# Choosing the step of a 64-row tile by where a run of score banks stands, and short runs in the first block

## The chip, the cores and the metric

One core of a Trainium2 chip runs the whole program. The metric is the time of one execution on the device, in microseconds (us), lower is better. Each kernel was run several times beside the kernel before on the same chip.

Words used throughout: **PE** is TensorE, **ACT** ScalarE, **DVE** VectorE. A *step* is the use of one key group (four tiles of 128 keys) for one query *block* (512 queries, six blocks in a batch, six steps in a block, eight batches, 288 steps). A *score unit* is half a group: two 64-row matmuls into one pair of PSUM banks, one ACT pass (relu and scale), one DVE square. A *run* is the score units issued one after the other within a step. The *tail* is the last key tile, which has only 64 rows. *Mixer work* is the MLP of the batch before, filled in between.

## The reference, cut to what matters

```python
scores = (1 / S) * z @ z.T                      # S = 3008, 64 features
attn   = maximum(scores, 0) ** 2
x      = u * (attn @ v)                         # 3008 x 256 for each of 8 batches
u2     = x + (relu(x.T @ w_tok1) @ w_tok2).T    # token mixing
out    = u2 + relu(u2 @ w_ch1) @ w_ch2          # channel mixing
```

Scores are symmetric: outside the first batch only key groups g >= q are computed ("direct"), the others come from a transposed copy.

## The kernel before: the parts that matter

Scores contract over 64 rows, so two matmuls share the array on its two halves. The tail does the same: its two output halves are computed side by side from the two copies of 64 rows. Everything else uses all 128 rows.

```python
BURST = 3
def burst(us):                      # a run: score matmuls on PE, then ACT; returns the squares
    for (b, q, g), pr in us:
        sc = psum.tile([P, 2, QW], F32, tag="ps", name="sc", bufs=3)
        for r in range(2):          # two 64-row matmuls, one on each half of the array
            nc.tensor.matmul(sc[:, r, :W], zT[h, ...], zT[h, ...])
    ...
    nc.scalar.activation(view, sv, ACT.Relu, scale=inv_S)
    return [lambda u=u, v=v: square(u, v) for u, v in zip(us, views)]   # DVE

def key_order(b, q):                # before: the tail's group (NG-1) has a fixed place
    direct = [g for g in range(NG) if direct_block(b, q, g)]
    if q == 0:
        return direct if b == 0 else [direct[0], direct[-1]] + direct[1:-1]
    direct = [direct[-1]] + direct[:-1]
    ...                             # then direct and transposed groups in turn

for n, (b, q, g) in enumerate(groups):
    def due(used):                  # are the next groups' scores running short?
        return ahead < len(units) and ahead < (used + 2) * (GK // 2)
    used += direct_block(b, q, g)
    if n and due(used):
        squares = burst(units[ahead:ahead + BURST]); ahead += BURST
    pre, half = av(b, q, g, first, last)
    for f in pre: f()               # the tail pair, if this is the tail's group
    if n and not last:
        for f in squares: f()
    half(0)                         # products into accumulator 0
    if last: gate(b, q, 0)          # DVE: accumulator 0 times u
    ...                             # mixer work
    half(1)                         # products into accumulator 1
    if last:
        gate(b, q, 1)
        for f in squares: f()       # in a block's last step the squares stand behind both gates
    ...
```

## Time and profile before

| | before |
|---|---|
| median of 4 runs (lowest to highest) | 1239.66 us (1238.43 to 1240.38) |
| PE busy | 97% of the span |
| DVE / ACT busy | 49% / 40% |
| granted PE clock, mean | 0.996 |

PE is the bound. Its busy time cannot be read as work, because a matmul's end is modelled and a 0.38 us bar covers the short waits behind it. I go by the time from one matmul's start to the next one's.

### The profile page before, as it was taken

Reading aid. Unit: us, or ns where it says so; the run is one execution under the profiler, and the core shown is the slowest. Engines: PE = TensorE matmul, PEld = TensorE weight load, DVE = VectorE, ACT = ScalarE, POOL = GpSimd, SP = SyncE. Lnnn points to the kernel's source line nnn. Section 1 sums busy time; section 2 is a strip of 40 time slices with the busy share of each in tenths; the row PEclk is TensorE's granted clock in tenths of the full one; section 3 lists DMA queues with packets and bytes.
Section 4 is the critical chain, followed back from the end, with each engine's and each line's share of the span. In section 5 each row is a group of like instructions: output and inputs, shape, how many; then the busy total and the mean of one; then the engine's idle time right before and its main releaser. Section 6 shows DMA issues by size and latency. Waiting matters only on the chain.

```text
span 1238.4 us, 17322 instructions
## 1 busy us (share of the span) xinstructions
PE 1198.6 (97%) x7089; PEld 631.8 (51%) x7089; DVE 605.8 (49%) x781; ACT 493.8 (40%) x521; POOL 144.4 (12%) x272
## 2 busy tenths in 40 slices
PE   6999999999999999999999999999999999999998
PEld 2334455554555555464545545555455554555566
DVE  3665644436444365435454355543653436443443
ACT  4776443333433334323443244423434334332022
POOL 2542010110101001011001111011010110000000
PEclk8999999999999999999999999999999999999999
DMA  8999955897657967689576876578965897544132
GB/s 140 139 140 171 159 113 105 141 163 146 110 119 132 173 118 133 123 132 175 103 125 128 157 137 125 114 148 154 147 112 102 147 165 139 110 85 86 33 77 67
DMA packets 438400, 157.73 MB, mean 127 GB/s; under 512 B 402288, under 2 KB 415920, under 8 KB 438320
## 3 DMA queue, kind: packets, MB, share of 16 engines
q1 hardware_dynamic: 410464, 123.92, 52.5%
q0 software_dynamic: 27344, 32.32, 19.0%
q8 instruction: 55, 0.90, 0.3%
q10 hardware_dynamic: 512, 0.38, 0.1%
q14 instruction: 25, 0.20, 0.1%
HBM read 65.40 MB, written 24.64 MB: 73 GB/s over the span
## 4 chain that ended last, share of the span: by engine, by line
PE 79%; ACT 9%; DVE 5%; issue 4%; DMA 3%; SPq 0%; POOL 0%; DVEq 0%; ACTq 0%; POOLq 0%
PE acc L304 34%; PE hp L393 18%; PE op L411 18%; ACT at L260 6%; PE sc L242 5%; DVE xT L376 3%; ACT h2pre L400 3%; PE a_ps L358 3%; DMA zT<-zr 1%; DVE xT L330 1%; DMA u_sb<-xT 1%; DMA fl<-at 1%; PE h_ps L372 1%; DVE h2pre L398 0%; DMA x_sb<-xT 0%
## 5 line engine op out<-in xcount | busy, mean ns | idle before, releaser
L260 ACT ACTIVATE at<-sc 128x1024 bf16<-128x1024 f32 (+1 forms) x366 | 342.9, 1023 | 369.0 <-PE sc L242 369.0
L304 PE MATMUL acc<-at,v_sb 128*128 128x512 bf16 (+3 forms) x1464 | 359.2, 380 | 6.3 <-DVE xT L330 5.4
L265 DVE TENSOR_TENSOR at<-at 128x1024 bf16<-128x1024 bf16 (+1 forms) x366 | 250.2, 701 | 209.8 <-ACT at L260 208.1
L304 PEld LDWEIGHTS <-v_sb 128*128 128x128 bf16 (+1 forms) x2304 | 208.0, 98 | 270.9 <-issue 77.9
L411 PE MATMUL op<-w_ch_sb,h2pre 128*128 128x256 bf16 (+1 forms) x2304 | 277.9, 273 | 5.9 <-ACT h2pre L400 2.8
L400 ACT ACTIVATE h2pre<-hp 128x1024 bf16<-128x1024 f32 (+1 forms) x144 | 145.1, 1007 | 314.6 <-PE hp L393 314.6
L393 PE MATMUL hp<-xT,w_ch_sb 128*128 128x512 bf16 (+1 forms) x1152 | 266.8, 375 | 2.6 <-ACT h2pre L400 2.3
L411 PEld LDWEIGHTS <-h2pre 128*128 128x128 bf16 (+1 forms) x2304 | 223.1, 98 | 66.1 <-ACT h2pre L400 13.0
L398 DVE TENSOR_SCALAR h2pre<-hp 128x1024 bf16<-128x1024 f32 (+1 forms) x144 | 171.8, 1199 | 77.9 <-PE hp L393 77.5
L304 PE MATMUL acc<-fl,v_sb 128*128 128x512 bf16 (+1 forms) x840 | 193.5, 370 | 0.0
L393 PEld LDWEIGHTS <-w_ch_sb 128*128 128x128 bf16 x1152 | 112.6, 98 | 133.1 <-issue 5.6
L419 DVE TENSOR_TENSOR res<-op,u_sb 128x512 f32<-128x512 f32 x88 | 60.9, 692 | 222.4 <-PE op L411 184.1
L242 PE MATMUL sc<-zT 64*128 64x512 bf16 (+1 forms) x732 | 107.4, 381 | 16.3 <-DMA zT<-zr 7.2
L330 DVE TENSOR_TENSOR xT<-acc,uT 128x512 bf16<-128x512 f32 (+1 forms) x96 | 63.9, 668 | 70.9 <-PE acc L304 69.6
L242 PEld LDWEIGHTS <-zT 64*128 64x128 bf16 x732 | 30.1, 94 | 94.4 <-issue 72.4
L147 POOL DMA_DIRECT2D ur<-in_u_dram x48 | 26.0, 543 | 419.2 <-DMA uT<-ur 411.5
L97 POOL COPY zr<-zs 128x512 bf16<-128x512 bf16 x42 | 27.0, 644 | 343.6 <-DMA zT<-zr 343.3
L376 DVE TENSOR_TENSOR xT<-xT,h_ps 128x1024 bf16<-128x1024 bf16 (+1 forms) x48 | 53.9, 1192 | 14.0 <-PE h_ps L372 14.0
L372 PE MATMUL h_ps<-w_tok_sb,a_sb 128*128 128x512 bf16 (+1 forms) x192 | 43.3, 374 | 1.5 <-ACT a_sb L364 0.7
L358 PE MATMUL a_ps<-x_sb,w_tok_sb 128*128 128x256 bf16 x384 | 43.7, 273 | 1.0 <-DMA x_sb<-xT 1.0
L137 POOL DMA_DIRECT2D v_sb<-in_v_dram x48 | 25.9, 543 | 143.7 <-PE acc L304 136.8
L358 PEld LDWEIGHTS <-w_tok_sb 128*128 128x128 bf16 x384 | 37.6, 98 | 7.6 <-issue 1.2
(34 smaller groups left out, 115.3 us busy)
## 6 DMA issues: line engine op xcount, KB each, us to landing
out_dram<-res SPq DMA_DIRECT2D x88, 256.0 KB, 2.3
v_sb<-in_v_dram POOLq DMA_DIRECT2D x40, 256.0 KB, 5.3
ur<-in_u_dram POOLq DMA_DIRECT2D x40, 256.0 KB, 5.6
zs<-in_z_dram POOLq DMA_DIRECT2D x35, 64.0 KB, 4.0
fl<-at SPq DMA_TRANSPOSE x105, 4.6
v_sb<-in_v_dram POOLq DMA_DIRECT2D x8, 192.0 KB, 5.1
w_ch_sb<-in_moe_w_ch_dram POOLq DMA_DIRECT2D x4, 384.0 KB, 5.6
ur<-in_u_dram POOLq DMA_DIRECT2D x8, 192.0 KB, 3.3
```

Of the source, the lines that this page charges most:

```text
L242: nc.tensor.matmul(sc[:, r, :W], zT[h, k * P:(k + 1) * P], zT[h, q * QW:q * QW + W], start=True, stop=True)
L260: nc.scalar.activation(view, sv, ACT.Relu, scale=inv_S)
L265: nc.vector.tensor_mul(view, view, view)
L304: nc.tensor.matmul(o, vt[rows, i, dh * P:(dh + 1) * P], rhs, start=st, stop=sp, skip_group_check=True)
L330: nc.vector.tensor_mul(xT[:, dh, :full * P].rearrange("p (t s) -> p t s", s=P), acc[:, :full * P].rearrange("p (t s) -> p t s", s=P), uT[: ...
L358: nc.tensor.matmul(st["a_ps"][:, th, :], w_tok1_sb[:, k, th * P:(th + 1) * P], x[:, :, i, :], start=(k == 0 and th == 0), stop=(k == KT - ...
L376: nc.vector.tensor_add(xT[:, :, :W], xT[:, :, :W], h[:, :, :W])
L393: nc.tensor.matmul(hp[:, r, :W], w_ch1_sb[:, dc, cc * P:(cc + 1) * P], xT[:, dc, :W], start=(dc == 0), stop=(dc == DT - 1))
L398: nc.vector.tensor_single_scalar(h2[:, :, :W], hp[:, :, :W], 0.0, AX.max)
L400: nc.scalar.activation(h2[:, :, :W], hp[:, :, :W], ACT.Relu)
L411: nc.tensor.matmul(op[:rows[i], i, :], st["h2", q, cc // 2][:, cc % 2, c0:c0 + rows[i]], w_ch2_sb[:, cc, :], start=(cc == 0 and i == 0), s ...
L419: nc.vector.tensor_add(res.rearrange("p i (h d) -> p i h d", d=P), op.rearrange("p i (h d) -> p i h d", d=P), us[:, :, half * 2:half * 2 + ...
```

## The change

Its intent: PE pays for each change between 128-row and 64-row use, so put the tail directly behind a run of score matmuls, which is in 64-row mode already. For that the tail's group loses its fixed place: it is taken at the first step where its two units have been issued and a run is due. The first block gets runs of two, so that a run does not ask for a key group whose z has not arrived. Core of the diff, with cuts marked:

```diff
+    def made(b, q):                 # order in which the score units are made
+        gs = [g for g in range(LAST) if direct_block(b, q, g)]
+        return gs if (b, q) == (0, 0) else gs[:1] + [LAST] + gs[1:]
...
-    for f in burst(units[:BURST]):
+    for f in burst(units[:2]) + burst(units[2:4]):
         f()
...
-    ahead = BURST
+    ahead = 4
...
+    def choose(n, used):
+        b, q = n // NB, n % NB // NG
+        todo = left.setdefault((b, q), key_order(b, q) + [LAST])
+        if n < NG:
+            return todo[0], 0 < n
+        tail = (b, q, LAST)
+        if LAST in todo and place[tail] * 2 + 2 <= ahead and due(used + 1):
+            return LAST, True
+        return todo[0], due(used + direct_block(b, q, todo[0]))
...
-        if n and due(used):
-            squares = burst(units[ahead:ahead + BURST])
-            ahead += BURST
+        if now:
+            size = 2 if n < NG else BURST
+            squares = burst(units[ahead:ahead + size])
+            ahead += size
...
-        if n == 0:
-            for f in burst(units[ahead:ahead + BURST]):
-                f()
-            ahead += BURST
```

The buffer of squared scores also goes from five to six copies, and the scores of the tail's group are as a rule made second in their block.

More of the change, by code (lines that the diff above doesn't have):

```diff
@@ L208, in direct_block @@
         return b == 0 or g >= q
+    LAST = NG - 1
+    def made(b, q):
+        gs = [g for g in range(LAST) if direct_block(b, q, g)]
+        return gs if (b, q) == (0, 0) else gs[:1] + [LAST] + gs[1:]
     def key_order(b, q):
-        direct = [g for g in range(NG) if direct_block(b, q, g)]
-        if q == 0:
-            return direct if b == 0 else [direct[0], direct[-1]] + direct[1:-1]
-        direct = [direct[-1]] + direct[:-1]
-        flipped = [g for g in range(NG) if not direct_block(b, q, g)]
+        direct = [g for g in made(b, q) if g < LAST]
+        flipped = [g for g in range(LAST) if not direct_block(b, q, g)]
         order = []
@@ L222, in key_order @@
         return order
-    groups = [(b, q, g) for b in range(B) for q in range(NQ) for g in key_order(b, q)]
-    directs = [t for t in groups if direct_block(*t)]
+    directs = [(b, q, g) for b in range(B) for q in range(NQ)
+               for g in made(b, q) + ([LAST] if (b, q) == (0, 0) else [])]
+    place = {t: i for i, t in enumerate(directs)}
     units = [(t, pr) for t in directs for pr in range(GK // 2)]
@@ L249, in burst @@
             if pr == 0:
-                ats[b, q, g] = sb.tile([P, GK * QW], BF16, tag="at", name="at", bufs=5)
+                ats[b, q, g] = sb.tile([P, GK * QW], BF16, tag="at", name="at", bufs=6)
             at = ats[b, q, g]
@@ L453, in new_zT @@
         zTs[b] = sb.tile([P, KT, P], BF16, tag="zT", name="zT", bufs=2)
-    vorder = key_order(1, 0)
+    vorder = [0, LAST] + list(range(1, LAST))
     new_zT(0)
@@ L535, in mix, with due @@
             budget -= w.cost
-    for n, (b, q, g) in enumerate(groups):
+    NB = NQ * NG
+    left = {}
+    def due(used):
+        return ahead < len(units) and ahead < (used + 2) * (GK // 2)
+    def choose(n, used):
[7 more added lines that the diff above has]
+        return todo[0], due(used + direct_block(b, q, todo[0]))
+    for n in range(B * NB):
+        b, q = n // NB, n % NB // NG
         for f in fetch.get(n, []):
@@ L541 @@
         t = 1.73
-        def due(used):
-            return ahead < len(units) and ahead < (used + 2) * (GK // 2)
+        g, now = choose(n, used)
+        left[b, q].remove(g)
         squares = []
         used += direct_block(b, q, g)
-        if n and due(used):
-            squares = burst(units[ahead:ahead + BURST])
-            ahead += BURST
+        if now:
+            size = 2 if n < NG else BURST
+            squares = burst(units[ahead:ahead + size])
+            ahead += size
             t += 0.42 * BURST * 0.8
@@ L553 @@
         got = budget
-        soon = n + 1 < len(groups) and due(used + direct_block(*groups[n + 1]))
+        soon = n + 1 < B * NB and choose(n + 1, used)[1]
         pre, half = av(b, q, g, first, last)
```

## The prediction

> **What bounds the kernel now.** I read the page first (busy shares, slices, groups), then the groups kept apart by shape, then the timeline at three places: the start, and two steps at which the group with the 64-row tile is used.
>
> ```profile
> PE 1198.6 (97%) x7089; PEld 631.8 (51%) x7089; DVE 605.8 (49%) x781; ACT 493.8 (40%) x521; POOL 144.4 (12%) x272
> ...
> PE   6999999999999999999999999999999999999998
> ```
>
> TensorE is busy 97% of the span in program order; VectorE and ScalarE are half idle. Only the first slice (31 us) has a visible hole. So time is gained only where TensorE waits or works badly, and any wait put into its stream is paid in full. Modelled ends hide short waits, so I go by start-to-start times: a warm 512-column matmul follows another after 0.216 us, a 448-column one after 0.189, a pair of 64-row matmuls on the two halves costs one such time.
>
> ```profile
> 643.36 1.03 PE L393 MATMUL hp<-xT,w_ch_sb 128*128 128x512 bf16 x4
> 644.32 1.14 PE L304 MATMUL acc<-at,v_sb 64*128 64x512 bf16 x5
> 645.30 1.03 PE L393 MATMUL hp<-xT,w_ch_sb 128*128 128x512 bf16 x4
> ```
>
> The tail (two 64-row matmuls side by side) with three full matmuls behind it. Four full matmuls should take 0.864 us; 643.36 to 644.32 is 0.96, so the way into 64-row mode costs 0.096. From 644.32 to 645.30 one pair and three matmuls should again be 0.864 and take 0.98: the way back costs about 0.1. **A run of 64-row matmuls costs about 0.195 us besides its work.** Single records say the same: 0.312 instead of 0.216 going in, 0.305 to 0.319 coming out.
>
> The second cost stands where the tail opens a query block. It writes both accumulators at once; the second is free only when the previous block's second gate (L330) is done.
>
> ```profile
> 577.84 0.69 DVE L330 TENSOR_TENSOR xT<-acc,uT 128x512 bf16<-128x512 f32 x1 [0.73 <-PE acc L304]
> 578.60 0.10 PEld L304 LDWEIGHTS <-v_sb 64*128 64x128 bf16 x2 [0.42 <-issue]
> 578.71 0.69 DVE L330 TENSOR_TENSOR xT<-acc,uT 128x512 bf16<-128x512 f32 x1 [0.17 <-PE acc L304]
> 579.31 1.89 DVE L265 TENSOR_TENSOR at<-at 128x1024 bf16<-128x1024 bf16 x3
> 579.45 1.34 PE L304 MATMUL acc<-at,v_sb 64*128 64x512 bf16 x5 [0.46 <-DVE xT L330]
> ```
>
> No score run stands here. The first tail matmul starts with its weights at 578.60, its partner at 579.45: 0.85 us lost. Only now do the **squares** of the previous step's run start (579.31): in the last step of a block the program puts them behind both gates.
>
> ```profile
> 168.24 0.82 PE L242 MATMUL sc<-zT 64*128 64x512 bf16 x6
> 168.35 0.69 DVE L330 TENSOR_TENSOR xT<-acc,uT 128x512 bf16<-128x512 f32 x1 [0.17 <-PE acc L304]
> ...
> 168.90 1.32 PE L304 MATMUL acc<-at,v_sb 64*128 64x512 bf16 x5
> 168.95 3.09 DVE L265 TENSOR_TENSOR at<-at 128x1024 bf16<-128x1024 bf16 x5
> ```
>
> Here a run of three banks comes first and hides most of the gate: the tail pair is 0.19 us apart. Five squares take 3.09 us: 0.60 start to start, 0.68 for the last one.
>
> **What the Trainium skill says.** "TensorEngine Tiling (Array Packing)", Key Properties: changing the tiling mode drains the TensorE. The trace agrees: 0.096 in, about 0.1 out. "TensorE: Matmul & The Clock Gate", Part 1, on engine queue depths, and Part 2, step 1: matmuls keep program order and the vector engine is a strict FIFO, so a tail that waits holds all behind it and a square cannot pass a gate; the two timelines agree. The same page, Part 1 on the clock gate: an idle array falls to half its clock after about 3.4 us. After the 7.16 us wait in the start below, eight matmuls take 3.5 us (20.70 to 24.22), twice the warm 1.73.
>
> **The change, part by part.**
>
> (a) Fewer mode switches. I walked both schedules through by hand. There are 366 score units (72 in the first batch, 42 in each other). Before: one opening run, 120 steps with a run, and 27 of the 48 tails in a step without one: 148 stretches. After: one opening stretch, 123 steps with runs (the first block has runs of two), and a lone tail only in the very last block: 125. 23 x 0.195 = **4.5 us saved**, all on TensorE's path.
>
> (b) Gate waits. Before, from the single records: five in batch 0 (four of 0.85, one 0.84 with a late first accumulator), seven of 0.85 (block 1 of batches 1 to 7), thirteen of 0.19 and one of 0.38 (blocks 2 and 5): 12.8 us. After, nearly every tail opens its block behind a run of three, so each pays 0.19: four in batch 0, 36 in batches 1 to 6, four and one of about 0.63 (a run of one bank) in batch 7: 44 x 0.19 + 0.63 = 9.0. **3.8 us saved.**
>
> (c) A new wait, on the squares. The tail is now taken as soon as its two score units have been *issued*, without asking whether they are squared. At step 42 (batch 1, block 1) the group is 43 in the making order, so units 86 and 87; 89 have been issued, so it is chosen. But 86 to 88 were issued in step 41, the last of block 0, where the squares stand behind the gates. By the walk that happens at 19 tails: blocks 2 to 5 of batch 0, block 0 of batch 1, blocks 1 and 3 of each later batch; always the run's second unit is the needed one. Before, no tail has a lag below two steps except in the first block. Cost, by the rows at 168: gate starts 168.35, its squares would run 168.95 and 169.55, the second ends at 170.24, the tail could start at 170.29. Without this it starts at 168.90, its partner at 169.09. So 1.2 us on top of the 0.19: 19 x 1.2 = **22.8 us added**.
>
> (d) The start.
>
> ```profile
> 11.69 0.39 PE L242 MATMUL sc<-zT 64*128 64x512 bf16 x2 [0.69 <-ACT at L260]
> 12.61 0.39 PE L242 MATMUL sc<-zT 64*128 64x512 bf16 x2 [0.52 <-ACT at L260]
> 20.15 0.61 PE L242 MATMUL sc<-zT 64*128 64x512 bf16 x2 [7.16 <-DMA zT<-zr]
> 20.70 3.60 PE L304 MATMUL acc<-at,v_sb 128*128 128x512 bf16 x8
> 24.22 1.46 PE L242 MATMUL sc<-zT 64*128 64x512 bf16 x6
> ```
>
> A run of three at step 1 already needs key group 4, whose turned z lands at 20.1; the products of groups 1 to 4 stand behind it. With runs of two, step 3 is the first to need it, so groups 1 and 2 (16 matmuls, 3.5 us warm) fall into the wait. Against it: the casts for chunks 4 and 5 wait for a fourth square, about 1 us later, though the transfer also stands among 1.8 MB of other loads; I allow 0.5. I put the tail of the first block at 28.1 instead of 32.8: 4.7 us. Four score units fewer are made by then (4 x 0.22 = 0.9), and step 6 meets the wait of (c) once more (1.3). **2.5 us saved**, give or take 2.
>
> The sixth buffer for squared scores costs no time. Sum: -4.5 - 3.8 + 22.8 - 2.5 = +12.0, so 1240.3 + 12.0 = 1252; I say **1251**, as some waits may partly fall on others.
>
> **Rivals.** *The intended gain only.* If the squares were done in time, (c) falls away: 1240.3 - 10.8 = about 1229, 0.9% faster. For it: VectorE is 49% busy. Against it: the wait is one of order, not load; the squares visibly start after the second gate at 168.95 and 579.31. *Scalar engine as the bound in the first blocks:* three banks per step take 2.8 us there (2.85 for three), more than the 2.4 to 2.6 of a step without mixer work; for steps 6 to 9 that could add 1 to 2 us, 1253. *The start gives nothing:* if key group 4 lands a few us later because its casts slip, (d) is zero: 1254. *Gates later than I think:* mixer work with a 1.2 us VectorE operation ahead of the gate could add 0.3 us at some 30 blocks: up to 1260.
>
> **Range and chances.** 1242 to 1258: the low end is about half of (c) hidden, the high end no gain at the start plus some late gates. Faster by 2% needs 1215, more than all savings together: 0.01. Slower by 2% needs 1265, twice the net loss: 0.03. Within 2%: 0.96.
>
> **What will show it.** (a) 125 stretches of 64-row matmuls, nearly every tail directly behind a score run. (b) Tail pairs about 0.19 us apart where nothing else is awaited. (c) A new group of waits, the tail (L304 in the old numbering) on the square (L265 there), some 19 times and 1.2 to 1.4 us each, with two squares between gate and tail. (d) Two more groups of products before 20 us. What would make me wrong: the squares' order on VectorE differing from the program's, or a landing of group 4 that moves by many us.

## The result, and the profile after

The changed kernel takes **1239.98 us** (median of 4, 1238.77 to 1240.19) against 1239.66 before: ratio 1.0002, interval 0.9984 to 1.0019. Nothing was gained or lost, where I had written 1251.

The page of the changed kernel, busy times (lines of the program have moved: L304 is now L311, L265 L272, L242 L249, L330 L337):

```profile
PE 1185.6 (96%) x6998; PEld 634.0 (51%) x7089; DVE 602.5 (49%) x781; ACT 494.5 (40%) x521; POOL 145.9 (12%) x272
```

PE records are 6998 where its weight loads are 7089: 91 matmul records are missing in this trace, none in that of before. The lower busy time is therefore no gain.

Waits of PE, before and after (total us, number, longest). Before:

```profile
PE sc L242 <- DMA zT<-zr: 7.2, 1, 7.2
PE acc L304 <- DVE xT L330: 5.4, 12, 0.5
```

After:

```profile
PE acc L311 <- DVE at L272: 20.9, 22, 1.4
PE sc L249 <- DMA zT<-zr: 5.2, 1, 5.2
```

The waits on the gate (xT) are gone from the list and waits on the squares (at) stand in their place, 20.9 us of them: part (c) of the prediction is there. One of them in the timeline of the changed kernel (start, length, engine, line, operation, output<-inputs, count):

```profile
576.81 1.14 PE L249 MATMUL sc<-zT 64*128 64x512 bf16 x6
576.91 0.69 DVE L337 TENSOR_TENSOR xT<-acc,uT 128x512 bf16<-128x512 f32 x1 [0.17 <-PE acc L311]
...
577.52 3.09 DVE L272 TENSOR_TENSOR at<-at 128x1024 bf16<-128x1024 bf16 x5
...
578.86 1.79 PE L311 MATMUL acc<-at,v_sb 64*128 64x512 bf16 x8 [0.91 <-DVE at L272]
```

Read it downwards: the run (576.81), the second gate (576.91), the squares (from 577.52, one each 0.60), and the tail only at 578.86, when two squares are done.

The start of the changed kernel, PE alone, to be set against the start shown in the prediction:

```profile
13.96 1.90 PE L311 MATMUL acc<-at,v_sb 128*128 128x512 bf16 x7
21.06 1.03 PE L249 MATMUL sc<-zT 64*128 64x512 bf16 x4 [5.20 <-DMA zT<-zr]
22.03 3.36 PE L311 MATMUL acc<-at,v_sb 128*128 128x512 bf16 x8
25.33 0.61 PE L249 MATMUL sc<-zT 64*128 64x512 bf16 x4
...
28.48 1.79 PE L311 MATMUL acc<-at,v_sb 64*128 64x512 bf16 x8 [0.17 <-DVE at L272]
```

Key group 4 arrives 0.9 us later (21.06 for 20.15), two groups of products stand ahead of it (one of them at 13.96), and the first block's tail starts at 28.48, where the prediction had 28.1.

**A ledger of lost time.** For every pair of neighbouring matmul records I took the time between their starts, less the pure streaming time of the first one (columns / 2400 + 0.0026 us, which gives the measured 0.216 and 0.189; 0.004 within a pair on two halves). The rest is lost time. Up to 0.1 us at a change of mode is booked as *mode*, what is left goes to the kind of the second matmul. An interval that is too long by exactly one matmul is a missing record and is taken out; those at a mode change or a wait slip through, 1 to 2 us in the changed kernel. A real wait of about that length is taken out with them (without this step the kernel before, which misses no record, has about 100 us), so read the differences and not the sums. The first 36 us are booked as a whole (*start*).

| us lost | before | after | difference | predicted |
|---|---|---|---|---|
| start | 16.9 | 13.9 | -3.0 | -2.5 |
| mode changes (284 and 234 of them) | 27.1 | 22.2 | -4.9 | -4.5 |
| tail waits: gates and squares | 11.8 | 29.1 | +17.3 | +19.0 |
| waits of score matmuls | 14.1 | 10.4 | -3.7 | 0 |
| waits of the second channel matmuls | 10.6 | 7.3 | -3.3 | 0 |
| other waits (products, token, first channel) | 9.2 | 9.0 | -0.2 | 0 |
| after the last step | 4.9 | 4.4 | -0.5 | 0 |
| sum | 94.6 | 96.3 | +1.7 | +12.0 |

The +1.7 is zero within the missing records. The rows that I had worked out come out near their predictions (for the start that is partly luck, as an experiment below shows). They add to +9.4; what I had left at zero gives most of it back. A place where the score waits shrink is block 0 of a batch, before:

```profile
262.00 0.82 PE L242 MATMUL sc<-zT 64*128 64x512 bf16 x6
262.43 5.61 ACT L260 ACTIVATE at<-sc 128x1024 bf16<-128x1024 f32 x6 [12.87 <-PE sc L242]
...
262.66 1.78 PE L304 MATMUL acc<-at,v_sb 64*128 64x512 bf16 x8
...
264.37 0.60 PE L242 MATMUL sc<-zT 64*128 64x512 bf16 x4
...
265.34 0.39 PE L242 MATMUL sc<-zT 64*128 64x512 bf16 x2 [0.36 <-ACT at L260]
```

and after:

```profile
256.83 0.82 PE L249 MATMUL sc<-zT 64*128 64x512 bf16 x6
...
257.27 2.85 ACT L267 ACTIVATE at<-sc 128x1024 bf16<-128x1024 f32 x3 [10.87 <-PE sc L249]
...
257.49 3.78 PE L311 MATMUL acc<-at,v_sb 64*128 64x512 bf16 x15
...
261.21 0.82 PE L249 MATMUL sc<-zT 64*128 64x512 bf16 x6
```

Before, two runs stand 2.4 us apart, ACT needs 2.8 us for three units, and the third unit of the second run waits for a bank (0.52 us by the single records, in each of seven batches). After, there are 4.4 us between the runs and nothing waits. So runs had *moved*, and with them the mixer work, which the program places by whether a step holds a run. Two readings were open. **P (places):** where runs of three fall against the groups of two decides a set of small waits, and the change moved all runs (and the mixer work between them). **S (slack):** the long tail waits let ACT and DVE catch up, so later waits shrink; then the tail waits cost little by themselves.

### The profile page after: what moved, and what is told of

The parts are those of the page before. It is cut to its first block, busy times and chain, and to the rows that moved or that the text cites. A ratio compares the mean times of both kernels' runs of the same rounds, so it can differ in the third digit from the quotient of the medians.

```text
span 1238.4 us, 17193 instructions
## 1 busy us (share of the span) xinstructions
PE 1185.6 (96%) x6998; PEld 634.0 (51%) x7089; DVE 602.5 (49%) x781; ACT 494.5 (40%) x521; POOL 145.9 (12%) x272
## 4 chain that ended last, share of the span: by engine, by line
PE 82%; ACT 7%; DVE 6%; issue 3%; DMA 2%; DVEq 0%; POOL 0%; ACTq 0%; SPq 0%
PE acc L311 36%; PE op L418 19%; PE hp L400 18%; PE sc L249 5%; ACT at L267 4%; PE a_ps L365 3%; ACT h2pre L407 3%; DVE at L272 2%; DVE xT L383 2%; PE h_ps L379 1%; DMA zT<-zr 1%; DVE h2pre L405 1%; DVE xT L337 1%; DMA ur<-in_u_dram 1%; DMA uT<-ur 0%
## 5 line engine op out<-in xcount | busy, mean ns | idle before, releaser
L311 PE MATMUL acc<-at,v_sb 128*128 128x512 bf16 (+3 forms) x1437 | 354.8, 379 | 23.1 <-DVE at L272 20.9
L311 PEld LDWEIGHTS <-v_sb 128*128 128x128 bf16 (+1 forms) x2304 | 212.2, 98 | 281.0 <-issue 73.3
L272 DVE TENSOR_TENSOR at<-at 128x1024 bf16<-128x1024 bf16 (+1 forms) x366 | 247.2, 699 | 168.6 <-ACT at L267 166.6
L418 PEld LDWEIGHTS <-h2pre 128*128 128x128 bf16 (+1 forms) x2304 | 223.4, 98 | 63.5 <-ACT h2pre L407 10.4
L311 PE MATMUL acc<-fl,v_sb 128*128 128x512 bf16 (+1 forms) x813 | 192.6, 370 | 1.4
L249 PE MATMUL sc<-zT 64*128 64x512 bf16 (+1 forms) x732 | 105.0, 379 | 11.8 <-DMA zT<-zr 5.2
L337 DVE TENSOR_TENSOR xT<-acc,uT 128x512 bf16<-128x512 f32 (+1 forms) x96 | 63.7, 668 | 75.3 <-PE acc L311 74.1
L249 PEld LDWEIGHTS <-zT 64*128 64x128 bf16 x732 | 28.6, 94 | 85.9 <-issue 65.8
L383 DVE TENSOR_TENSOR xT<-xT,h_ps 128x1024 bf16<-128x1024 bf16 (+1 forms) x48 | 53.9, 1193 | 15.1 <-PE h_ps L379 15.1
```

What stands on the lines that cost most here:

```text
L249: nc.tensor.matmul(sc[:, r, :W], zT[h, k * P:(k + 1) * P], zT[h, q * QW:q * QW + W], start=True, stop=True)
L272: nc.vector.tensor_mul(view, view, view)
L311: nc.tensor.matmul(o, vt[rows, i, dh * P:(dh + 1) * P], rhs, start=st, stop=sp, skip_group_check=True)
L337: nc.vector.tensor_mul(xT[:, dh, :full * P].rearrange("p (t s) -> p t s", s=P), acc[:, :full * P].rearrange("p (t s) -> p t s", s=P), uT[: ...
L383: nc.vector.tensor_add(xT[:, :, :W], xT[:, :, :W], h[:, :, :W])
L418: nc.tensor.matmul(op[:rows[i], i, :], st["h2", q, cc // 2][:, cc % 2, c0:c0 + rows[i]], w_ch2_sb[:, cc, :], start=(cc == 0 and i == 0), s ...
```

## The experiments

### Are the tail waits paid in full?

**Squares ahead of the second gate.** Only the DVE order in a block's last step changes.

```diff
+            for f in squares[:2]:
+                f()
             gate(b, q, 1)
-            for f in squares:
+            for f in squares[2:]:
                 f()
```

> The changed kernel, with only the order on VectorE altered: in the last step of a block the first two squares stand ahead of the second gate instead of behind it. Theory A (the square wait costs what it shows; the rest of the expected gain was offset elsewhere by better-placed score runs): the 19 tail waits of 1.3 to 1.8 us in the trace fall to 0.2 to 0.5 us, the tail waits as a whole from 29 us to about 10, and the time falls by about 19 to 22 us, to 1218 to 1221. Rival B (the tail waits only took the place of waits for ScalarE and VectorE that PE would have paid later anyway): the tail waits fall as above but waits of score and channel matmuls grow back by 8 us or more, and the time falls by less than 12 us, to 1228 or more.

Measured: **1235.97 us** (4 runs, ratio to before 0.9976). The tail waits fell from 29.1 to 24.9 us only; I had expected 10. The timeline of block 1 in batch 2 shows why: the squares start at 274.03, right behind the first gate (273.42), and the second gate comes at 275.23. They have just changed places in DVE's queue, and the tail needs both. Most of the 19 tails gained some 0.27 us this way. So the edit was a weak one. But what it took from the tail waits, 4.2 us, came off the time (1239.98 to 1235.97), and the waits of score and second channel matmuls stayed (10.5 and 7.3). By its time alone the run lies where I had put S (1228 or more); but S also needed the tail waits to fall to 10 and the other waits to grow back by 8, and neither happened. That speaks for P, weakly.

**The tail never in a block's first step.**

```diff
-        if LAST in todo and place[tail] * 2 + 2 <= ahead and due(used + 1):
+        if n % NG and LAST in todo and place[tail] * 2 + 2 <= ahead and due(used + 1):
```

> The changed kernel, with the tail forbidden in the first step of a block, so that neither gates nor late squares stand before it; 40 of 48 tails still follow a score run, 132 stretches of 64-row matmuls in place of 125. Theory A: tail waits of 29 us fall to about 1, seven more stretches cost 7 x 0.195 = 1.4, so about 1213. Rival B: less than 14 us gained, 1226 or more.

Measured: **1219.52 us** (ratio to before 0.9838, interval 0.9821 to 0.9854), the fastest kernel by a little. The tail waits are gone (29.1 to 0), 20.5 us came off. This edit also moves runs, and new waits of 3.6 us appear before the first channel matmuls, so it is not a clean test, but S expected less than 14.

**The tail one step later, every run where it was.** The changed kernel's plan is worked out first; where it opens a block with the tail, the tail and the group behind it trade steps.

```diff
+    for n in range(0, B * NB, NG):
+        if plan[n][0] == LAST:
+            plan[n][0], plan[n + 1][0] = plan[n + 1][0], LAST
...
-        g, now = choose(n, used)
+        g, now = plan[n]
```

> The changed kernel with each score run in its own step as it is, but where the tail opens a block it trades steps with the group behind it. The runs keep their places, the tail waits (29 us) go, 38 more mode switches come (163 stretches in place of 125, 38 x 0.195 = 7.4). If the smaller waits of score and channel matmuls come from the places of the runs: they stay near 10.4 and 7.3 us and the time is 1240 - 29 + 7.4 = 1218. If they are small only because the waiting tails let the other engines catch up: they grow back by 7 us or more and the time is 1225 or above.

Measured: **1220.44 us** (ratio 0.9850). Tail waits 29.1 to 0.2, mode changes 22.2 to 29.6 (as the sum of 38 x 0.195 said), score waits 10.2, second channel waits 8.4: they did not come back. Its waits of PE on the squares and for banks, to be set against 20.9 us of the first kind in the changed kernel's list (and 2.4 us, 5 times, of the second):

```profile
PE sc L249 <- ACT at L267: 2.0, 5, 0.9
...
PE acc L311 <- DVE at L272: 1.0, 3, 0.6
```

This is the clean one, and S falls: the waits at the tail cost what they show, and the small waits are low because of where the runs stand.

**One more wait.** An extra DVE operation of a square's size between the second gate and the squares.

```diff
             gate(b, q, 1)
+            nxt = (n + 1) // NB, (n + 1) % NB // NG
+            if soon and n > NG and choose(n + 1, used)[0] == LAST and place[nxt + (LAST,)] * 2 + 2 > ahead - BURST:
+                nc.vector.tensor_mul(dum[:], dum[:], dum[:])
```

> The changed kernel with one more VectorE operation of a square's size (0.60 us start to start) between the second gate and the squares, only at the 19 steps whose next step takes a tail that needs those squares. Theory A: each is paid in full, 19 x 0.60 = 11.4 us more, 1251. Rival B: as PE's later waits shrink in return, half of it or less, 1246 or below.

Measured: **1257.39 us**, +17.4, more than any theory said. My condition was faulty: it also fired in 26 blocks in whose last step no run stands, 45 in all (DVE operations 826 for 781). The corrected condition adds `squares and`:

> The earlier try with one more square-sized VectorE operation hit 45 block ends instead of 19: its condition did not ask whether a run stood in that step. Corrected here to the blocks whose last step holds a run with the tail's squares. If the tail waits are paid in full: 0.60 us at each, 11 to 12 us more than the changed kernel, 1251 to 1252. If later waits shrink in return: 1246 or below.

Measured: **1259.40 us** (median of 5, 1256.21 to 1263.24; ratio to before 1.0163), with 800 DVE operations, so 19 extra ones. The tail waits rose by 12.3 us (29.1 to 41.4), near 19 x 0.60 = 11.4, and no other wait shrank. But the time rose by 19.4. The rest is the PE clock, which the timeline shows at one of these steps:

```profile
961.55 0.91 PE L249 MATMUL sc<-zT 64*128 64x512 bf16 x6
...
962.53 0.68 DVE L604 TENSOR_TENSOR dum<-dum 128x1024 bf16<-128x1024 bf16 x1
...
963.12 3.69 DVE L272 TENSOR_TENSOR at<-at 128x1024 bf16<-128x1024 bf16 x6
964.46 1.28 PE L311 MATMUL acc<-at,v_sb 64*128 64x512 bf16 x5 [2.01 <-DVE at L272]
...
965.53 2.77 PE L400 MATMUL hp<-xT,w_ch_sb 128*128 128x512 bf16 x6
```

Six matmuls take 2.77 us here; at full clock six would show 1.46 (5 x 0.216 and the 0.38 of the last one's bar). By windows of the same trace (stretch, its length, busy time of PE, PEld, DVE, ACT and POOL, then the granted clock, DMA share and GB/s):

```profile
963.00:965.00 2.00, 0.54 (x3) 0.21 (x3) 2.00 (x5) 1.83 (x3) 0.00 (x0) 1.00 0.64 120
965.00:967.00 2.00, 2.00 (x7) 0.80 (x6) 1.82 (x4) 0.00 (x0) 0.00 (x0) 0.59 0.80 151
965.40:968.70 3.30, 3.30 (x9) 1.22 (x8) 1.42 (x3) 1.02 (x1) 0.00 (x0) 0.50 0.84 159
```

The array stood idle for 2.0 us up to 964.46, and from 965.35 the granted clock was half for 3.41 us. The clock record of this trace has five such spells after the start, at 50.6, 200.8, 658.2, 965.4 and 1119.0, each 0.5 to 0.9 us behind the end of a tail wait of 1.99 us or more (eight tail waits are that long); between the start and the last step the changed kernel, whose longest tail wait is 1.58, has none. Five times half of 3.41 is 8.5 us, which covers the 7.1 that the tail waits leave (19.4 - 12.3). Over the whole run the clock was 0.990, against 0.997 in the changed kernel. So a tail wait is paid in full, and some of the longer ones more than once. S is out.

### What is the start worth, and what does it move?

**The first block long again, the new tail rule kept.**

```diff
-    for f in burst(units[:2]) + burst(units[2:4]):
+    for f in burst(units[:BURST]):
...
-            size = 2 if n < NG else BURST
+            size = BURST          # and again a run behind step 0
```

> The changed kernel with the first block's score runs as before (three banks, a second run behind step 0, the order of everything else kept). The start then waits for key group 4 with four groups of products behind it. My prediction: 2.5 to 3.0 us slower than the changed kernel, 1242.5 to 1243. Rival (the start gains nothing that reaches the end): within 1 us of 1240.

Measured: **1251.34 us** (4 runs), 11.4 slower than the changed kernel; both expectations miss. The start accounts for 0.5 us of it in the ledger. The tail waits even fell, from 29.1 to 14.0. The waits of PE in this run:

```profile
PE acc L311 <- DVE at L272: 11.9, 7, 2.0
PE sc L249 <- ACT at L267: 11.7, 21, 1.1
...
PE h_ps L379 <- DVE xT L383: 5.7, 7, 0.8
```

In the ledger, score waits are 18.2 (for 10.4), token waits 10.6 (2.0), first and second channel waits 7.2 and 10.1 (3.9 and 7.3), products 5.2 (3.1). The edit had changed more than the start. With the old start 18 units are made by step 6, with the short one 14. From then on each run takes three units while each group needs two. Counted in threes, 18 and 15 are the same position of the runs against the groups; 14 is another. With another position *every later run of the program* falls due in other steps and holds other halves of groups. I call this the **shift**. The mixer work between the runs moves with them; no run parts the two.

**The old start, but 14 units by step 6.**

```diff
-            return todo[0], 0 < n
+            return todo[0], 0 < n < 4
...
-            size = 2 if n < NG else BURST
+            size = 2 if n == 3 else BURST    # old opening runs: 3, 3, 3, 3, 2
```

> The changed kernel with the start's runs as before (three banks ahead of step 0, three behind it, three at step 1, then three and two), but 14 units made by step 6 as in the changed kernel, so that every later run holds the same banks. This parts the start from what the earlier try mixed with it (there, later runs held other banks and the time rose by 11 us). Theory: the start alone is worth 2.5 to 3.5 us, so 1242.5 to 1243.5. Rival: the start is worth the 11 us, 1249 to 1251.

Measured: **1241.22 us** (5 runs, ratio to before 1.0014), 1.2 us slower than the changed kernel. In the ledger every item is within 0.2 us of the changed kernel's, the start too (13.9 us in both). So the start itself is worth 0 to 1.2 us, less than the 2.5 that I had predicted, and far from 11. This also means that the -3.0 of the ledger's start row does not hang on the short runs: with the old opening runs under the new rule it is there, or nearly (13.9 here and 14.4 in the experiment before this one, against 16.9 in the kernel before). In both of these runs key group 4 is there at 18.8 to 18.9 us, in the kernel before at 20.15; why is open.

**The short start alone in the kernel before.**

```diff
-        if n and due(used):
-            squares = burst(units[ahead:ahead + BURST])
+        if 0 < n < NG or n and due(used):
+            size = 2 if n < NG else BURST
+            squares = burst(units[ahead:ahead + size])
```

> The kernel before with the first block's short runs alone; the order of the groups stays. Later runs then hold other banks (14 made by step 6 instead of 18). If only the start counted: 3 us faster, 1236.5. If which banks a run holds matters by several us, as the earlier try of the opposite suggests: off from that by 4 us or more, either way, with the difference in waits of tails, score, token and channel matmuls.

Measured: **1224.90 us** (1221.43 to 1226.34; ratio 0.9881). The start alone, without the new tail rule, gains 14.6 us. With the fixed order of before, the shifted runs meet 40 of the 48 tails by themselves (21 before), 132 stretches of 64-row matmuls in place of 148. Block 1 of batch 2 in this run, a kind of block in which the prediction showed the tail paying 0.85 us for the gate:

```profile
272.10 1.14 PE L242 MATMUL sc<-zT 64*128 64x512 bf16 x6
273.07 1.79 PE L304 MATMUL acc<-at,v_sb 64*128 64x512 bf16 x8
```

The tail now follows a run, and nothing is waited for between them (the run's own length, 1.14 us for 0.82, holds a wait of 0.3 us for a bank).

**The short start, with the old position.** One unit more than in the last experiment: 15 by step 6.

```diff
-            size = 2 if n < NG else BURST
+            size = 2 if n < NG - 1 else BURST
```

> The kernel before with the short start, but 15 units made by step 6: the same position of the runs of three against the groups of two as before (18 units), so the start without the shift. If the shift makes the 14.6 us that the short start alone gained: nearly nothing is left, 1 to 3 us faster than before, 1236.5 to 1238.5. If the start itself makes them: 1225.

Measured: **1236.53 us** (5 runs, ratio 0.9984, interval 0.9971 to 0.9996): 2.1 us faster than the kernel before of the same rounds. One unit in the first block makes the difference between 1236.5 and 1224.9. The ledger after the start is that of before, item by item (tail waits 11.8, score 14.1, second channel 10.6). Between these two kernels mode changes and tail waits give 3.5 us each (26.9 to 23.4 and 11.8 to 8.3, table below), so 7.0 of the 11.6 us come from tails that now meet a run, and most of the rest from score (1.9) and second channel waits (2.8).

**The other positions.** The fastest kernel (tail not in the first step) with 15 and with 16 units by step 6, and the kernel before with 16 (edits as above, with `NG - 1` and `NG - 2`).

> The changed kernel with the tail forbidden in a block's first step (1219.5 us), and one more unit made in the first block (15 by step 6), so that every later run holds other banks. If the banks' phase counts by several us: off from 1219.5 by 4 us or more. If not: within 2 us.

> The changed kernel with the tail forbidden in a block's first step, and 16 units made by step 6 (14 gave 1219.5, 15 gave 1258 us): the third and last position that runs of three can have against the groups of two. If the position counts by several us, as those two say, this one differs from 1219.5 by 4 us or more; if 15 was a single bad case, within 3 us of 1219.5.

> The kernel before with a short start that makes 16 units by step 6 (before: 18, that is the same position as 15, 1239.5 us; with 14: 1224.9). By the order of the steps 34 of 48 tails then follow a run, 137 stretches, against 40 and 132 with 14, and 21 and 148 before. If the position acts mainly by joining tails to runs, this lies between the two, 1226 to 1233; if the other waits dominate, it can lie outside them.

| units by step 6 | before's order | tail not in first step |
|---|---|---|
| 14 | 1224.90 | 1219.52 |
| 15 (18 alike) | 1236.53 (1239.5 with the old start) | 1255.42 (1251.26 to 1260.73, 3 fast runs) |
| 16 | 1227.91 (1219.41 to 1232.29) | 1246.20 (1243.43 to 1251.72) |

The position counts by up to 12 us in the order of before and up to 36 in the other. In the order of before the times do follow the stretches (132, 137 and 148), and the kernel with 16 lies at 1227.91, where I had put it if tails joined to runs were the main effect. In the other order they do not: 15 units has the fewest stretches (125, against 132 with 14 and 131 with 16) and is the slowest. In the run with 15 and the tail not first, one waits line stands out:

```profile
PE a_ps L365 <- DMA x_sb<-xT: 16.8, 5, 6.0
```

Token matmuls now stand before the transposed x has landed, up to 6.0 us each, and the mean clock fell to 0.992. With 16 units the same line is 11.0 us in one wait, and 4.6 us in one in the order of before. Why each position has just its set of waits I have not followed up one by one, nor why the fast runs of three of these kernels spread by 8 to 13 us; that stays open.

### The ledger of the main kernels

| us lost | start | mode | tail | score | products | token | channel 1 | channel 2 | time |
|---|---|---|---|---|---|---|---|---|---|
| before | 16.9 | 27.1 | 11.8 | 14.1 | 4.1 | 2.0 | 3.1 | 10.6 | 1239.7 |
| short start, 15 units | 15.0 | 26.9 | 11.8 | 14.1 | 4.1 | 2.0 | 3.1 | 10.6 | 1236.5 |
| short start, 14 units | 15.1 | 23.4 | 8.3 | 12.2 | 4.0 | 2.0 | 3.7 | 7.8 | 1224.9 |
| the change | 13.9 | 22.2 | 29.1 | 10.4 | 3.1 | 2.0 | 3.9 | 7.3 | 1240.0 |
| the change, first block long | 14.4 | 22.2 | 14.0 | 18.2 | 5.2 | 10.6 | 7.2 | 10.1 | 1251.3 |
| the change, tail one step later | 13.7 | 29.6 | 0.2 | 10.2 | 7.9 | 2.0 | 4.2 | 8.4 | 1220.4 |
| the change, one more wait | 13.8 | 22.2 | 41.4 | 10.5 | 4.4 | 2.0 | 9.6 | 7.1 | 1259.4 |

(Products in the sixth row hold some 4 us of missing records. The last row's channel 1 is high because its matmuls run at a lowered clock.)

From the four corners of the change: with the old position the tail rule costs 1251.3 - 1239.7 = 11.6, with the new one 1240.0 - 1224.9 = 15.1. The short start, mostly by its shift, gains 14.8 under the old rule (1239.7 - 1224.9) and 11.3 under the new. The change is the sum of two parts of a dozen us or more each, with opposite signs.

## Why the prediction was wrong

It said 1251, range 1242 to 1258; 1239.98 lies below the range.

- **(a) Mode changes:** -4.5 predicted, -4.9 in the ledger. Right in mechanism and size. (Either part alone gives much of it: the short start in the kernel before brings 27.1 to 23.4, the rule with the first block long 27.1 to 22.2.)
- **(b) and (c), gate and square waits:** +19.0 predicted, +17.3 found. The new wait is where I put it, at the 19 tails named. At the seven tails of block 1 it is 1.08 us for 1.39, because the run itself waits 0.3 us for a bank first; at seven of the other twelve it is 1.39 or more. Right in mechanism, slightly too large. (The waits listed under (b) for the kernel before add to 13.0, not 12.8; the ledger has 11.8 after the start.)
- **The tail rule as a whole,** (a) + (b) + (c), was put at +14.5. Measured alone: +11.6 to +15.1.
- **(d) The start, the step that failed.** I wrote: "Four score units fewer are made by then (4 x 0.22 = 0.9)", and counted them as work put off. They are not: 14 in place of 18 moves every later run against the groups. The start itself is worth 0 to 2.1 us, but with the shift the short start gains 14.8 under the old rule and 11.3 under the new. Part of that gain I had booked in (a) and (b), since I walked both schedules. What I had not booked is that the waits of score, product and channel matmuls would change with the runs' places: -3.7, -1.0 and -2.5 in the ledger (channel: +0.8 before the first and -3.3 before the second matmuls), and -0.5 after the last step, -7.7 in all. I had left them at zero without saying so. That the position makes them is seen in the table above: under the new rule the waits of score, product, token and channel matmuls are 51.3 us with the old position (first block long) and 26.7 with the new; under the old rule they are 33.9 (15 units) and 29.7 (14 units). That the start row came to -3.0 for my -2.5 is luck, since the old opening runs give it too.
- **The rivals.** "The intended gain only" and "gates later than I think" did not happen. "The start gives nothing" was near for the start itself, though for another reason. No rival of mine said that waits that I had not looked at could *fall*; my range was built from the terms I had, with nothing for those I had not.
- **The chances** (0.96 for within 2%) held, but the range was too narrow on its low side by 2 us.

The expectation of the first try at the start missed in the same way (1242.5 to 1243 for 1251.34).

## What to carry to other kernels

When a change alters how much is made ahead, ask first whether it shifts the phase of everything that follows, and test it with a neighbour that differs by one unit: here one unit in the first 30 us of 1240 was worth 12 us. A rule that uses work as soon as it has been *issued* must ask whether it is *finished*, and behind what its last operation stands in its engine's queue. And a sum over the terms one has looked at needs a term for the waits one has not, of either sign.

## What the Trainium skill lacked or had wrong

- "TensorEngine Tiling (Array Packing)", Key Properties, names the drain at a change of tiling mode but gives no cost. Here it is 0.096 us into 64-row mode and 0.09 to 0.10 us back, the same for score matmuls and for the tail, at 0.216 us for a matmul of 512 columns.
- "TensorE: Matmul & The Clock Gate", Part 1, has the clock fall after an idle window of about 3.4 us. In the run with one more wait, 2.0 us of idle array (962.45 to 964.46) were followed, from 965.35, by half the clock for 3.41 us and matmuls 0.427 us apart. The array was busy up to that gap, so here a wait well below 3.4 us was enough; of eight tail waits of 1.99 us or more, five were followed by such a spell. 12.3 us more of tail waits made this run 19.4 us slower.
